# A gated mix of two attentions: Q, K and the output projected over dense features, with heads moved through DRAM

## The chip, the cores and the metric

The kernel runs on one core of one Trainium2 chip. A core has a matrix engine (PE, with a weight load that overlaps it, PEld), a vector engine (DVE), a scalar engine (ACT), a general engine (POOL) and SyncE (SP), which here only issues transfers; 16 DMA engines move the data. Each engine takes its instructions in order. The metric is the device time of one execution in microseconds (us). Before the change the median of three runs is 1757.69 us (1755.98 to 1764.59).

## The reference

Two attentions read the same `x` (2048 tokens, 640 features), and a gate mixes their outputs:

```python
g = sigmoid((x * gate_w).sum(-1, keepdims=True))
a = A_ref(x, mem0, Wq, Wk, Wv, Wo, seg_len)   # recurrent, 32 heads of 192
b = B_ref(x, wqkv, wo)                        # sliding, 32 heads of 20
out = g * a + (1 - g) * b
```

A cuts the tokens into 64 segments of 32. Each segment has 8 memory tokens in front; all 40 tokens are projected to q, k and v (640 to 6144 each), 32 heads attend with a causal mask, and the output projection gives 32 rows of the result and the next segment's 8 memory tokens. So the segments are serial.

B projects q, k, v (640 to 640 each, 32 heads of 20). Each token attends to 8 keys, its own and those 2, 4, ... 14 positions back; then comes a 640 by 640 output projection.

## The kernel before

The program has four stages: Part B (`part_b`, from L90), the prepass (L414), Part A (L509) and a last stage (L855) that finishes the rows the memory recurrence set aside. Everything is bf16 with sums in f32.

**Part B** works on the tokens in five blocks b: four of 484 and one of 112, each with 14 halo tokens in front. A block has eight steps g, each for four heads. The main loop (L296 to L331) runs through the steps (b, g) and calls:
- `make_xT(b)` (L159): transposes 512 tokens of x on PE, evicts them to `xT`, makes the gate g, copies tokens on POOL into `xh_blk` (stored to DRAM for Part A) and into `zTi`, the first eight tokens per segment, which the prepass reads. It runs at g = 2 of the block before.
- `make_v(b)` (L203): V of a block in four position groups u (two parities, two halves); at g = 6 of the block before.
- `proj(b, g)` (L220): q and k of four heads, with the features on partitions and the tokens along the row. [...] It is called one step ahead.
- `scores(b, g)` (L234): per two heads, matmuls over the 32 rows of a head (`ps_bS`), one exponential on ACT (L249), one multiplication with the band mask on DVE (L253).
- `values(b, g)` (L256), one step behind: `ps_bO`, the weighted sums, and `ps_bZ`, the sums of the weights; ACT takes logarithm and exponential of the latter (L271, L272: the reciprocal), DVE multiplies (L274) into `OT`, again 32 rows per head.
- `out_tile(ti)` (L277): output projection of 128 tokens over the eight groups of padded rows, in two halves of eight matmuls, scaled by 1 - g and stored to DRAM (`bsc_dram`). It is called from g = 1 on, when the tokens are complete.

Transposes, gate, V, q/k and the output share two PSUM banks (pool `psm`); the scores have two double banks and `psO` one bank each for O and Z. The pool `wk` gives two buffers unless a call says otherwise.

**The weights of Part A** are 80 slices of 384 KB (128 x 1536). `N_STREAM` = 14 of them are streamed anew in each segment. Of the rest, `N_EARLY` = 23 are loaded in Part B (`load_early`, L376, which also copies the 20 output slices into a contiguous DRAM buffer `wscr`), after the first `xh_blk` store. The others follow in four groups as memory becomes free (`load_late`, L399): after Part B, before the fourth q/k pass (4), before the V rounds (8) and after the prepass (4).

**The prepass** projects the 512 recurrent tokens for all segments at once and writes them to DRAM (`zpk_dram`): four passes for q and k (L434, 96 groups of five matmuls of 128 x 512), then V in four rounds of four tiles, each with 15 matmuls into three PSUM banks (L446), three evictions and two stores. `load_late(2)` (L463) puts eight slice loads on SP's queue before the first round.

**Part A** has its instruction order for PE, ACT and DVE written out by hand; for the rest, Tile's scheduler sets each engine's order from its own estimate. `load_z(s)` and `load_vz(s)` fetch one segment's prepass rows; both are issued by ACT. `load_vz(0)` stands before the loop (L544), and the later ones stand behind `store()`, after the fourth q/k group of the segment (L747).

A transfer signals one of eight semaphores that SP's and ACT's transfers use in turn; a transfer's issue waits until the one that used the semaphore before it has landed.

The functions that the change touches, with the line numbers that the profile uses:

Of the kernel before, what the change touches and what calls it, by code (L numbers as in the profile page):

```python
# [10 lines left out]
BF = mybir.dt.bfloat16  # L11
# [4 lines left out]
N_EARLY = 23  # L16
# [11 lines left out]
class _K:  # L28
# [61 lines left out]
    def part_b(self):  # L90
# [11 lines left out]
        with ExitStack() as ctx:  # L102
# [21 lines left out]
            wop = wp.tile([128, 8, 640], BF, name="wo_pad")  # L124
            wqk = [wp.tile([128, KC, 32, 32], BF, name=f"w{n}_pad") for n in "qk"]
            xT = wp.tile([128, KC, HALO + S], BF, name="xT")
            OT = wp.tile([128, 8, S], BF, name="OT")
            wsrc = self.wqkv.rearrange("(c p) f -> p c f", p=128)
            for n, w in enumerate(wqk):
                nc.gpsimd.memset(w[:, :, :, 20:32], 0.0)  # L130
                raw = OT[:].rearrange("p g t -> p (g t)")[:, 3200 * n:3200 * n + 3200]
                (nc.scalar, nc.sync)[n].dma_start(raw.rearrange("p (c f) -> p c f", c=KC), wsrc[:, :, 640 * n:640 * n + 640])
                for kc in range(KC):
                    eng = (nc.vector, nc.gpsimd)[(KC * n + kc) % 2]
                    eng.tensor_copy(w[:, kc, :, 0:20], raw[:, 640 * kc:640 * kc + 640].rearrange("p (h d) -> p h d", d=20))
            nc.sync.dma_start(gw[:], self.gate_w.rearrange("(c p o) -> p c o", p=128, o=1))
            nc.scalar.dma_start(wv[:], wsrc[:, :, 1280:1920])
            nc.gpsimd.memset(wop[:], 0.0)
            wosrc = self.wo.rearrange("(g h d) f -> h d g f", h=4, d=20)
            for hh in range(4):  # L140
                nc.sync.dma_start(wop[32 * hh:32 * hh + 20, :, :], wosrc[hh])
# [17 lines left out]
            def make_xT(b):  # L159
# [30 lines left out]
                with tc.issue_after(xh_store.ins):  # L190
                    nc.gpsimd.tensor_copy(zTi[:, :, :, 16 * b:16 * b + 16],
                                          xv[:, :, :, 24:32].rearrange("p s c i -> p c i s"))
                    if b == 3:
                        self.build_sel(self.const, sel_ones[:])
# [23 lines left out]
            qk = {}  # L218

            def proj(b, g):  # L220
                nq, nu, c0 = shape_of(b)
                nt = nq * nu
                for n, (o0, nn) in enumerate(((c0 + HALO, nt), (c0, nt + HALO))):
                    ps = bank(F32, "ps_bqk")
                    for kc in range(KC):
                        nc.tensor.matmul(ps[:, 0:nn], lhsT=wqk[n][:, kc, 4 * g:4 * g + 4, :].rearrange("p h d -> p (h d)"),  # L226
                                         rhs=xT[:, kc, o0:o0 + nn], start=(kc == 0), stop=(kc == KC - 1))
                    t = wk.tile([128, BQ + HALO], BF, name="b" + "qk"[n] + "T", bufs=3)
                    self.evac(t[:, 0:nn], ps[:, 0:nn], "dve" if n == 0 else "act")
                    qk[b, g, n] = t  # L230
# [3 lines left out]
            def scores(b, g):  # L234
                nq, nu, c0 = shape_of(b)
                nk = nq + 7
                qT, kT = qk.pop((b, g, 0)), qk.pop((b, g, 1))
                for hp in range(2):
                    ps = psS.tile([128, 2, 512], F32, tag="S", name="ps_bS")
                    for u in range(nu):  # L240
                        a = 242 * (u // 2) + u % 2
                        for r in range(2):
                            rs = slice(64 * hp + 32 * r, 64 * hp + 32 * r + 32)
# [12 lines left out]
            def values(b, g):  # L256
# [5 lines left out]
                for u in range(nu):  # L262
                    for out, z in ((pz, True), (po, False)):
                        for hh in range(4):
# [8 lines left out]
                dst = OT[:, g, BQ * b:BQ * b + nt].rearrange("p (l n q) -> p l q n", l=nu // 2, q=2)  # L273
                nc.vector.tensor_tensor(out=dst, in0=po[:, 0:nt].rearrange("p (l q n) -> p l q n", q=2, n=nq),  # L274
                                        in1=rz[:, 0:nt].rearrange("p (l q n) -> p l q n", q=2, n=nq), op=ALU.mult)

            def out_tile(ti):  # L277
                bo = io.tile([128, 640], BF, name="bo", bufs=2)
                for f in range(2):
                    ps = bank(F32, "ps_bo")  # L280
                    for g in range(8):
                        nc.tensor.matmul(ps[:, 0:320], lhsT=OT[:, g, 128 * ti:128 * ti + 128],
                                         rhs=wop[:, g, 320 * f:320 * f + 320], start=(g == 0), stop=(g == 7))
# [13 lines left out]
            with tc.issue_after(self.first_store):  # L297
                self.load_early()
            make_v(0)
            proj(*steps[0])  # L300
            ti = 0
            for i, (b, g) in enumerate(steps):
                if g == 2 and b + 1 < S // 512:
                    make_xT(b + 1)
                if (b, g) == (S // 512 - 1, 0):
# [12 lines left out]
                if g == 6 and i + 8 < len(steps):  # L318
                    make_v(b + 1)
                if i + 1 < len(steps):  # L320
                    proj(*steps[i + 1])
# [3 lines left out]
                if g >= 1 and b > 0 and 128 * (ti + 1) <= BQ * b:  # L325
# [25 lines left out]
    def weights_setup(self):  # L351
# [21 lines left out]
        self.ahead = {}  # L373
        self.wstream = self.ctx.enter_context(tc.tile_pool(name="wstream", bufs=WBUFS))

    def load_early(self):  # L376

        for k in self.early:
            self.res_tiles[k] = self.load_slice(self.wres, k, "wres_" + "_".join(map(str, k)))
        so = [k for k in self.slice_keys() if k[0] in ("oa", "ob") and k not in self.early]  # L380
        scr = self.dram.tile([len(so), 128, 1536], BF, name="wscr")
        for i, k in enumerate(so):
            src, split = self.slice_info(k)
            self.nc.sync.dma_start(scr[i].rearrange("p (c f) -> p c f", c=split[0]), src)
            self.wscr[k] = scr[i]

    def load_slice(self, pool, key, name, tag=None, t=None):
        src, split = self.slice_info(key)
        kw = {"tag": tag} if tag else {}
        if t is None:  # L390
            t = pool.tile([128, 1536], BF, name=name, **kw)
        v = t if split is None else t.rearrange("p (c f) -> p c f", c=split[0])
        if key in self.wscr:
            self.nc.sync.dma_start(t[:], self.wscr[key])
        else:
            self.nc.sync.dma_start(v[:], src)
        return v

    def load_late(self, part, side=None):  # L399
# [4 lines left out]
        for k in ks:  # L404
# [534 lines left out]
```

## Time and profile before

| what | value |
|---|---|
| median of three runs | 1757.69 us |
| profiled execution | 1761.81 us, span 1759.7 us, mean granted PE clock 0.993 |
| PE busy | 1675.3 us, 95% of the span |
| ACT, DVE, POOL busy | 872.1 (50%), 651.0 (37%), 71.3 (4%) us |
| first score matmul (L244) of blocks 0, 1, 2, 3, 4 | 31.45, 69.8, 118.3, 166.05, 207.2 us |
| first prepass matmul (L434) | 228.82 us |
| V rounds (L446), from first to last | 335.24 to 391.22 us |
| Part A's segments | from some 391 us on, about 21 us each |

The page gives the busy time of each engine and its share of the span; the chain of work that ended last, followed backward from the last instruction; and groups of instructions by line, engine, operation, output<-input and shape (partitions x elements), with their count, the busy time, the mean in ns, and the idle time before them with what ended it. Windows give the busy time of each engine in a stretch of the span, with the granted clock (1.00 is full) and the load of the DMA engines. PE pipelines its matmuls, so that the sum of their durations is more than the time they take; how far apart they start is read from the timeline.

### The profile page before, as it was taken

What the parts mean: (1) busy time and instruction counts of PE and PEld (TensorE: products, weight loads), DVE (VectorE), ACT (ScalarE), POOL (GpSimd) and SP (SyncE); (2) the same over time, 40 slices, a digit from 0 to 9 for tenths busy, and PEclk for the clock granted to TensorE, in tenths of its full rate; (3) what the DMA queues carried; (4) which work ended last, traced back from release to release, by engine and by line L of the source; (5) the groups of instructions that cost most, each with busy time, mean ns of one, the idle gap of its engine ahead of it and who ended that gap; (6) DMA issues with size and microseconds to landing.
All of it is one profiled execution on the core that took longest, in us unless ns stands there. A gap on an engine that the chain in (4) does not pass through costs nothing.

```text
span 1759.7 us, 82388 instructions
## 1 busy us (share of the span) xinstructions
PE 1675.3 (95%) x36512; PEld 998.3 (57%) x36527; DVE 651.0 (37%) x2065; ACT 872.1 (50%) x2377; POOL 71.3 (4%) x132
## 2 busy tenths in 40 slices
PE   6999999998999999999999999999999999999989
PEld 3555544445555555555555565556556655555557
DVE  4565533223333333333333333333333333333330
ACT  3766632224555555555555555555555555555550
POOL 6010000000000000000000000000000000000000
PEclk9999999999999999999999999999999999999999
DMA  6941184889999989999899999999999999998981
GB/s 172 332 125 33 40 294 120 219 248 314 298 304 293 291 282 304 308 300 304 293 295 307 298 296 308 305 297 299 304 297 306 307 297 299 301 303 296 297 286 30
DMA packets 280648, 466.50 MB, mean 265 GB/s; under 512 B 94820, under 2 KB 155748, under 8 KB 280292
## 3 DMA queue, kind: packets, MB, share of 16 engines
q1 hardware_dynamic: 178632, 401.83, 69.0%
q10 hardware_dynamic: 101660, 59.41, 11.7%
q8 instruction: 285, 4.67, 1.0%
q14 instruction: 71, 0.58, 0.1%
HBM read 427.47 MB, written 41.55 MB: 267 GB/s over the span
## 4 chain that ended last, share of the span: by engine, by line
PE 85%; ACT 6%; DMA 3%; issue 2%; DVE 2%; ACTq 0%; SPq 0%; DVEq 0%
PE ps_qk L560 25%; PE ps_v L653 13%; PE ps_wo L717 12%; PE ps_qkT L577 6%; PE ps_pre L434 6%; PE ps_S L607 5%; PE ps_oT L676 3%; PE ps_z L871 3%; PE ps_bqk L226 3%; ACT bP L249 2%; PE ps_pre L446 2%; ACT ZB L798 2%; PE ps_mem L727 1%; PE ps_bv L213 1%; PE ps_S L616 1%
## 5 line engine op out<-in xcount | busy, mean ns | idle before, releaser
L569 ACT CAST TZ<-ps_qk 128x384 bf16<-128x384 f32 x448 | 208.8, 481 | 332.3 <-PE ps_qk L560 185.5
L560 PEld LDWEIGHTS <-hT 128*32 128x32 bf16 x10240 | 246.8, 96 | 152.0 <-DVE hT L730 12.8
L584 DVE COPY ZB<-ps_qkT 128x384 bf16<-128x384 bf16 x256 | 91.6, 358 | 377.6 <-PE ps_qkT L577 212.3
L560 PE MATMUL ps_qk<-wres_q,hT 128*32 128x384 bf16 x4096 | 226.6, 328 | 2.8 <-issue 2.8
L653 PE MATMUL ps_v<-wlate_v,hT 128*32 128x384 bf16 x4096 | 224.8, 329 | 0.0
L717 PEld LDWEIGHTS <-TZ 128*32 128x32 bf16 x6144 | 154.6, 96 | 65.3 <-issue 17.4
L560 PE MATMUL ps_qk<-wlate_k,hT 128*32 128x384 bf16 x2560 | 159.8, 328 | 0.1
L560 PE MATMUL ps_qk<-wst,hT 128*32 128x384 bf16 x1792 | 153.1, 328 | 0.9 <-issue 0.7
L653 PEld LDWEIGHTS <-hT 128*32 128x32 bf16 x5120 | 113.4, 96 | 67.8 <-issue 5.1
L717 PE MATMUL ps_wo<-wlate_oa,TZ 128*32 128x384 bf16 x2560 | 140.8, 328 | 3.5 <-issue 3.4
L607 PE MATMUL ps_S<-ZB,TZ 128*128 128x160 bf16 (+1 forms) x1024 | 136.5, 237 | 0.8 <-issue 0.8
L577 PE MATMUL ps_qkT<-ident,TZ 128*128 128x128 bf16 x1536 | 130.2, 220 | 3.0 <-ACT TZ L569 2.2
L717 PE MATMUL ps_wo<-wlate_ob,TZ 128*32 128x256 bf16 x2688 | 124.5, 276 | 5.9 <-issue 5.9
L577 PEld LDWEIGHTS <-TZ 128*128 128x128 bf16 x1536 | 88.9, 98 | 64.0 <-issue 41.8
L560 PE MATMUL ps_qk<-wres_k,hT 128*32 128x384 bf16 x1792 | 119.8, 328 | 1.5 <-issue 1.1
L625 ACT ACTIVATE ZB<-ps_S 32x224 bf16<-32x224 f32 x256 | 89.4, 349 | 41.8 <-PE ps_S L616 38.7
L687 DVE CAST TZ<-ps_oT 128x192 bf16<-128x192 f32 x256 | 79.4, 351 | 61.9 <-PE ps_oT L681 61.9
L607 PEld LDWEIGHTS <-TZ 128*128 128x128 bf16 (+1 forms) x1024 | 58.8, 95 | 69.1 <-issue 41.5
L687 ACT CAST TZ<-ps_oT 128x192 bf16<-128x192 f32 x256 | 70.0, 328 | 56.1 <-PE ps_oT L681 56.1
L730 DVE CAST hT<-ps_mem 128x24 bf16<-128x24 f32 x126 | 22.5, 179 | 196.9 <-PE ps_mem L727 196.9
L660 ACT CAST TZ<-ps_v 128x384 bf16<-128x384 f32 x192 | 92.7, 483 | 3.1
L536 POOL COPY TZ<-ZB 128x384 bf16<-128x384 bf16 x64 | 32.5, 508 | 1514.4 <-DMA ZB<-zpk_dram 476.0
(142 smaller groups left out, 2443.7 us busy)
## 6 DMA issues: line engine op xcount, KB each, us to landing
wst<-in_A_Wq_dram SPq DMA_DIRECT2D x260, 384.0 KB
wst<-in_A_Wv_dram SPq DMA_DIRECT2D x260, 384.0 KB
wst<-in_A_Wk_dram SPq DMA_DIRECT2D x195, 384.0 KB
wst<-wscr SPq DMA_DIRECT2D x192, 384.0 KB
zpk_dram<-ZS ACTq DMA_DIRECT2D x4, 3072.0 KB
ZB<-zpk_dram ACTq DMA_DIRECT2D x64, 192.0 KB
wscr<-in_A_Wo_dram SPq DMA_DIRECT2D x20, 384.0 KB
wres_q<-in_A_Wq_dram SPq DMA_DIRECT2D x16, 384.0 KB
```

Source lines behind the costliest of these rows:

```text
L226: nc.tensor.matmul(ps[:, 0:nn], lhsT=wqk[n][:, kc, 4 * g:4 * g + 4, :].rearrange("p h d -> p (h d)"), rhs=xT[:, kc, o0:o0 + nn], start=(kc ...
L434: nc.tensor.matmul(ps[:], lhsT=sls[r][kc][:, c0:c0 + 128], rhs=zTi[:, kc, :], start=(kc == 0), stop=(kc == KC - 1))
L560: nc.tensor.matmul(pq[32 * j:32 * j + 32, 0:384], lhsT=hT[:, kc, :], rhs=sl[:, 384 * j:384 * j + 384], start=(kc == 0), stop=(kc == KC - 1 ...
L569: cp(sts[i], pqs[i][:, 0:384])
L577: nc.tensor.transpose(pT[:, t, :, :, :].rearrange("p j b i -> p (j b i)"), st[:, 128 * t:128 * t + 128], self.ident[:])
L584: nc.vector.tensor_copy(q_blocks(R)[:, 1:5, :, :].rearrange("p b c i -> p c b i"), pT.rearrange("p t j b i -> p (t j) b i"))
L607: nc.tensor.matmul(grid(h, par)[:, :, 0:80].rearrange("p j (b r i) -> p j b r i", r=2, i=8)[:, :, :, r, :], lhsT=KT[k0:k1, 12 * r + c:12 * ...
L625: nc.scalar.activation(E[ps], pSs[h][ps, :, 112 * j:112 * j + 112], ACT.Exp, scale=scale_a)
L653: nc.tensor.matmul(pvs[R][32 * j:32 * j + 32, 0:384], lhsT=hT[:, kc, :], rhs=sl[:, 384 * j:384 * j + 384], start=(kc == 0), stop=(kc == KC ...
L660: cp(V[R], pvs[R][:, 0:384])
L687: cps[j % 2](oTxs[2 * h + j // 2][:, 6 * (j % 2):6 * (j % 2) + 6, :], pos[j][:, 0:240].rearrange("p (c q) -> p c q", q=40)[:, :, 8:40])
L717: nc.tensor.matmul(pso[part][32 * jj:32 * jj + 32, 0:n], lhsT=oTxs[2 * (R // 2) + j // 2][:, 6 * (j % 2) + 3 * (R % 2) + t, :], rhs=o_weig ...
```

## The change

*Dense features.* The weights of q, k and the output projection are held as they come, [128, 5, 640]. `proj(b, f)` computes 128 dense features, f = 0 to 4, so a block needs 5 x 2 x 5 = 50 matmuls. A chunk of 128 features holds 6.4 heads; so that each head begins at a multiple of 32 partitions, the evicted chunk (`bqD`, `bkD`, two buffers each) is stored to a DRAM buffer, and after f = 2 and f = 4 eight loads bring half of the heads (16 heads, four steps) back as 32-row groups with 20 rows used (`bqT`, `bkT`, three buffers each). `scores` reads 20 rows. `values` writes into `boT`; after g = 3 and g = 7 four stores take it to DRAM, and after g = 7 one load brings the block's outputs back as dense features in `OT`. `out_tile` has 10 matmuls instead of 16.

*Order.* All five chunks of block 0 come before the first step; those of block b + 1 are called in steps 2 to 6 of block b. `make_xT` is called at g = 1, `make_v` at g = 7, `out_tile` from g = 3 on. The early loads are issued two per step instead of all at once, and there are 21 slices instead of 23; `wscr`'s copies follow them. POOL's copy into `zTi` no longer waits for the `xh_blk` store's issue.

*Late slices.* The eight loads of `load_late(2)` are issued one per V tile, from the fourth tile on, each after the tile's last matmul. The last four slices are issued in segment 0 after `m_qk(4)`. `load_vz` stands behind the fourth q/k group in segment 0 too.

```diff
-N_EARLY = 23
+N_EARLY = 21
...
-            wop = wp.tile([128, 8, 640], BF, name="wo_pad")
-            wqk = [wp.tile([128, KC, 32, 32], BF, name=f"w{n}_pad") for n in "qk"]
+            wo = wp.tile([128, KC, 640], BF, name="b_wo")
+            wqk = [wp.tile([128, KC, 640], BF, name=f"b_w{n}") for n in "qk"]
...
-                nc.gpsimd.memset(w[:, :, :, 20:32], 0.0)
...
-            nc.gpsimd.memset(wop[:], 0.0)
...
-            def proj(b, g):
+            heads = lambda t: t.rearrange("(g h d) n -> h d g n", h=4, d=20)
+            qk, qk_dram, ot_dram = {}, {}, {}
+
+            def proj(b, f):
...
+                    if f == 0:
+                        qk_dram[b, n] = self.dram.tile([640, nn], BF, name=f"b{'qk'[n]}_dram{b}")
                     ps = bank(F32, "ps_bqk")
                     for kc in range(KC):
-                        nc.tensor.matmul(ps[:, 0:nn], lhsT=wqk[n][:, kc, 4 * g:4 * g + 4, :].rearrange("p h d -> p (h d)"),
+                        nc.tensor.matmul(ps[:, 0:nn], lhsT=wqk[n][:, kc, 128 * f:128 * f + 128],
                                          rhs=xT[:, kc, o0:o0 + nn], start=(kc == 0), stop=(kc == KC - 1))
-                    t = wk.tile([128, BQ + HALO], BF, name="b" + "qk"[n] + "T", bufs=3)
+                    t = wk.tile([128, BQ + HALO], BF, name="b" + "qk"[n] + "D")
                     self.evac(t[:, 0:nn], ps[:, 0:nn], "dve" if n == 0 else "act")
-                    qk[b, g, n] = t
+                    nc.sync.dma_start(qk_dram[b, n][128 * f:128 * f + 128, :], t[:, 0:nn])
+                half = {2: 0, KC - 1: 1}.get(f)
+                if half is None:
+                    return
+                for n, nn in enumerate((nt, nt + HALO)):
+                    t = wk.tile([128, 4, BQ + HALO], BF, name="b" + "qk"[n] + "T", bufs=3)
+                    for hh in range(4):
+                        nc.sync.dma_start(t[32 * hh:32 * hh + 20, :, 0:nn],
+                                          heads(qk_dram[b, n][:])[hh][:, 4 * half:4 * half + 4, :])
+                    qk[b, half, n] = t
...
-                            rs = slice(64 * hp + 32 * r, 64 * hp + 32 * r + 32)
+                            rs = slice(64 * hp + 32 * r, 64 * hp + 32 * r + 20)
...
-                dst = OT[:, g, BQ * b:BQ * b + nt].rearrange("p (l n q) -> p l q n", l=nu // 2, q=2)
+                if g == 0:
+                    ot_dram[b] = self.dram.tile([640, nt], BF, name=f"bo_dram{b}")
+                if g % 4 == 0:
+                    ot_dram[b, "sb"] = wk.tile([128, 4, BQ], BF, name="boT")
+                oT = ot_dram[b, "sb"]
+                dst = oT[:, g % 4, 0:nt].rearrange("p (l n q) -> p l q n", l=nu // 2, q=2)
...
+                if g % 4 == 3:
+                    for hh in range(4):
+                        nc.sync.dma_start(heads(ot_dram[b][:])[hh][:, g - 3:g + 1, :], oT[32 * hh:32 * hh + 20, :, 0:nt])
+                if g == 7:
+                    nc.sync.dma_start(OT[:, :, BQ * b:BQ * b + nt], ot_dram[b][:].rearrange("(c p) n -> p c n", p=128))
...
-                    for g in range(8):
-                        nc.tensor.matmul(ps[:, 0:320], lhsT=OT[:, g, 128 * ti:128 * ti + 128],
-                                         rhs=wop[:, g, 320 * f:320 * f + 320], start=(g == 0), stop=(g == 7))
+                    for c in range(KC):
+                        nc.tensor.matmul(ps[:, 0:320], lhsT=OT[:, c, 128 * ti:128 * ti + 128],
+                                         rhs=wo[:, c, 320 * f:320 * f + 320], start=(c == 0), stop=(c == KC - 1))
...
-            with tc.issue_after(self.first_store):
-                self.load_early()
+            for f in range(KC):
+                proj(0, f)
             make_v(0)
-            proj(*steps[0])
-            ti = 0
+            early, ti = self.load_early(), 0
             for i, (b, g) in enumerate(steps):
-                if g == 2 and b + 1 < S // 512:
+                if g == 1 and b + 1 < S // 512:
                     make_xT(b + 1)
+                with tc.issue_after(self.first_store):
+                    for load in early[:2]:
+                        load()
+                del early[:2]
...
-                if g == 6 and i + 8 < len(steps):
+                if g == 7 and i + 1 < len(steps):
                     make_v(b + 1)
-                if i + 1 < len(steps):
-                    proj(*steps[i + 1])
+                if 2 <= g < 2 + KC and i + 8 < len(steps):
+                    proj(b + 1, g - 2)
...
-                if g >= 1 and b > 0 and 128 * (ti + 1) <= BQ * b:
+                if g >= 3 and b > 0 and 128 * (ti + 1) <= BQ * b:
...
+                if 4 * R + st >= 3 and loads:
+                    tc.add_manual_dep(loads.pop(0)().ins, mm.ins.name, self.after, reason="a load per tile")
...
-        self.load_late(2, "right")
+        loads = self.load_late(2, "right", wait=True)
...
-            load_vz(0)
...
                 if store is not None:
                     store()
-                    load_vz(s)
+                load_vz(s)
                 m_qk(4, range(KC))
+                if s == 0:
+                    for load in self.last_loads:
+                        load()
...
-    k.load_late(3)
+    k.last_loads = k.load_late(3, wait=True)
```

## The prediction

> **What bounds the kernel now.** I read the engine shares and the slices first, then the chain that ended last, and then, by windows, the stages that the change touches.
>
> ```profile
> PE 1675.3 (95%) x36512; PEld 998.3 (57%) x36527; DVE 651.0 (37%) x2065; ACT 872.1 (50%) x2377; POOL 71.3 (4%) x132
> ...
> PE 85%; ACT 6%; DMA 3%; issue 2%; DVE 2%; ACTq 0%; SPq 0%; DVEq 0%
> ```
>
> The matrix engine PE bounds the whole. Part B is the first 229 us; the table in front has its stages. Its mix, by groups of equal shape and by waits (us in total, times, longest), in 0 to 230 and 0 to 420 us:
>
> ```profile
> L249 ACT ACTIVATE bP<-ps_bS 128x968 bf16<-128x968 f32 x64 | 59.6, 985 | 0.1
> L226 PE MATMUL ps_bqk<-xT,wk_pad 128*128 128x498 bf16 x160 | 40.1, 382 | 1.0 <-ACT gz_sb L178 1.0
> L282 PE MATMUL ps_bo<-wo_pad,OT 128*128 128x320 bf16 x256 | 39.6, 304 | 0.6 <-DVE bqT L79 0.6
> L272 ACT ACTIVATE b_rz<-b_rz 128x484 f32<-128x484 f32 x32 | 19.6, 614 | 0.8
> L271 ACT ACTIVATE b_rz<-ps_bZ 128x484 f32<-128x484 f32 x32 | 19.0, 592 | 0.5 <-PE ps_bO L266 0.5
> L77 ACT CAST bkT<-ps_bqk 128x498 bf16<-128x498 f32 x32 | 18.3, 572 | 40.5 <-PE ps_bqk L226 40.5
> ...
> POOL xh_blk L185 <- DMA xh_dram<-xh_blk: 16.4, 1, 16.4
> ...
> ACT ZV L77 <- DMA wlate_ob<-wscr: 7.2, 1, 7.2
> ```
>
> Matmuls overlap, so a mean is not a price: in the timeline five projection matmuls start 1.03 us apart (205 ns each), sixteen output matmuls take 2.35 us (147 each), thirty V matmuls 4.36 (146). A plain step (66.2 to 69.9 to 73.3 us) takes 3.3 to 3.7 us: PE has 2.07 of projection, .36 of scores, .55 of values and the gaps between; ACT has two exponentials (1.86 from first start to last end), logarithm and exponential of rz (1.21) and the k eviction, some 3.5. Both are near their limit, so **PE work taken from a step does not shorten it unless ACT work goes too.** A step with an output tile takes 6.2 us (137.0, 143.2, 149.4), and there PE is the limit.
>
> Windows (PE, PEld, DVE, ACT, POOL busy; then the granted clock, DMA share, GB/s):
>
> ```profile
> 60.00:80.00 20.00, 18.64 (x307) 10.56 (x306) 12.44 (x25) 16.49 (x26) 0.00 (x0) 1.00 1.04 327
> 160.00:180.00 20.00, 17.95 (x267) 9.81 (x268) 12.99 (x23) 16.73 (x26) 0.00 (x0) 1.00 0.03 11
> ...
> 356.00:360.00 4.00, 2.25 (x11) 0.91 (x10) 1.29 (x2) 0.33 (x1) 0.00 (x0) 1.00 1.03 396
> 360.00:364.00 4.00, 3.69 (x10) 1.37 (x10) 0.01 (x1) 1.24 (x3) 0.00 (x0) 0.57 1.07 395
> ...
> 636.96:640.37 3.41, 1.93 (x85) 1.22 (x85) 0.85 (x4) 0.86 (x6) 0.00 (x0) 1.00 0.88 311
> 640.37:643.78 3.41, 3.41 (x58) 2.18 (x54) 0.18 (x1) 0.65 (x2) 0.00 (x0) 0.50 0.56 158
> ```
>
> See three things: the DMA engines are full early in Part B and empty after 140 us; PE is never under 88% in a plain stretch; and where PE was busy for only some 56% of 3 to 4 us, the next 3.41 us ran at half clock.
>
> **The change part by part.** *Removed from PE.* A full block projects with 50 matmuls instead of 80: 30 x .205 = 6.2 us; four blocks 24.6, the short block 30 x .06 = 1.8. Output: 96 of 256 matmuls x .14 = 13.4. Together 40 us. The shapes stay, so the rows are the same; score matmuls read 20 rows instead of 32, priced like L244's 32 (16 in .36; bounds .18 and .72, less than .4 us a step, under ACT's cover).
>
> *Removed elsewhere.* Per full block three k evictions on ACT (1.7 us) and three q evictions on DVE (2.0). The padding (memset L138 4.4 us and the rest on POOL, copies on DVE) lies before the first scores at 31.45; there now stand all five projections of block 0 (50 x .205 = 10.3 instead of one step's 2.1) on PE that waited for data anyway, and a trip through DRAM (7 us, below) that V's 5.8 us and the second half of the projections lie beside. I take 31.0; bounds 26 (the padding was the limit) and 38 (the trip without cover).
>
> *The order.* Compiled, the new program has PE's stream in two kinds: a block's eight head steps (scores, values) almost alone, with 10 or 20 projection matmuls between, then a lump of output, projection, V and transpose work. Before, each step carried its own projection. The walk, by rows:
> - heads: ACT 1.86 + 1.21 = 3.07 a step, eight steps 24.6. PE has .9 of this.
> - block 0: 24.6 + five k evictions 2.9 + trailing V and transposes (40 x .146 + 20 x .13 = 8.4, 1.5 beside the last step) + 4 of store waits (next part) = 38.4. Before 38.4.
> - block 1: 24.6 + .6 + lump (30 x .14 + 40 x .205 + 5.8 + 2.6 + .7 = 21.5) + 1 of store wait = 47.7. Before 48.5.
> - block 2: 24.6 + .6 + lump with ten more output matmuls 22.9 = 48.1. Before 47.8.
> - block 3: 24.6 + 1.1 + lump (40 output 5.6, short projections 1.8, short V 2.6, of which 2 beside heads) = 33.7. Before 41.2.
> - block 4 and the tail: ACT 8 x (.70 + .26 + .30) = 10 + 1.8 for its second half of q and k + 2 for the last output trip + 50 output matmuls 7.0 = 20.8. Before 21.6.
>
> Sum 31.0 + 38.4 + 47.7 + 48.1 + 33.7 + 20.8 = 219.7, so 9.1 below 228.8: of 40 us taken from PE three quarters only turn overlap into a sequence.
>
> *The clock.* A head step gives PE about .9 us of matmuls in 3.07, by the page's count (short ones overlap) 1.2, or 39%; with ten projection matmuls inside nearer 60%. The rows above go to half after 56%. So I expect half windows in the heads and at the start of each lump: .9 becomes 1.8 in a step that ACT holds at 3.07 (little), the first 3.41 us of a lump lose 1.7. I take 2 us in each of four blocks, 1 in the last: +9. Bounds: 0 and +25 (one in two windows of 125 us of heads at half, with PE work exposed each time for 1.3 us).
> [...]
>
> *Added: transfers.* Per block ten q/k stores, sixteen loads, eight stores and one load of outputs: 35 issues on SP at .33 to .45 us, 13 us of SP in a block of 40 (23 by the .66 of L312's sixteen): SP has room. The landing is what counts. Bounds for store plus dependent load: 3.8 us on an empty ring (store of g issued at 132.75, its reader at 136.54) and the 16.4 us that POOL waited for L187's store behind the resident loads, which come at one 384 KB slice per 1.0 us. From block 2 on (DMA share .03 to .2) the trip is 3.8 + 8 x .4, hidden a block ahead. In blocks 0 and 1 early slices, now two per step, share the ring; bqD and bkD have two buffers, so the third eviction waits for the first store, and DVE and ACT run in order: behind it are queued the band masks and the next exponentials, for which PE's values wait. I take 4 and 1 us; bounds 0 and 16.4 + 8. SP also waits, by the shared eight semaphores, for x loads that ACT issues; that is in the upper bound. Removing L190's ordering moves POOL's copy ahead by its store's issue, no price.
>
> *V rounds.* 335.24 to 391.22 is 56.0 us for 16 tiles of 3.24 = 51.8. Lost: 2.06 where PE waits at 358.25 for ACT's eviction, itself behind the late loads (7.2 us wait above), and 1.7 from the half window after it. Late loads released one per tile take that away: -3.5 (bounds -4.1 and +2: eight slices spread over tiles 3 to 10 are needed only in segment 0). Next late would be the streamed slices, for which PE waited 0 there. Two slices moved from early to late are 2 us of ring at 1.0 each, under the 106 us in which the prepass projects q and k, needed only after it: 0; without that cover 2.
>
> *Segment 0.* PE waits 2.22 us at 396.88 for an ACT copy held behind load_vz's issue (398.13); now that issue stands behind c_qk(3): -1.5. The wait of 1.96 for a streamed Wv slice at 405.95 stays or grows with two more late slices and the last four behind m_qk(4): bounds -2.2 and +4. The other 63 segments keep order and loads: 0, bounds ±0.1 each, as load_vz's place is the same there.
>
> Sum: -9.1 + 9 - 3.5 - 1.5 = **-5 us**. Profiled execution: 1761.8 - 5 = 1756.8; the median lies 4.1 below that execution, so **1753**.
>
> **The rivals.**
> *Forecast, no change that shows (chance .40):* 1753, 1748 to 1761.
> *Faster, full clock (.34).* Short bursts every step count as activity, or the lump overlaps with the next block's first heads. For it: the trace has seven half windows in all, though part A's 64 segments are full of short matmuls. Against: the 640.37 row. Then -9.1 - 5 = -14, 1743; with 6 us of lumps beside heads 1737.
> *Slower, store waits in blocks 0 and 1 (.18).* Third evictions wait for stores behind the resident slices. For it: the 16.4 us row. Against: loads are issued two per step, so at most some six lie ahead of a store. From 9 us beyond my 5 it cancels all; with two waits of 12 instead of 4 and 1, +19: 1772.
> *Slower, half clock throughout heads and lumps (.08).* The +25 bound: -14 + 25 = +11, 1769.
>
> **How the numbers follow.** A change under 0.5% (8.8 us) can't be told from none in this kernel. Faster: .34 and .02 from the forecast's edge, .36; slower .18 + .08 less .02 = .24; same .40. The range 1738 to 1772 leaves out a tenth on either side; the forecast's own is 1748 to 1761.
>
> **What would show it.** First scores at 31; blocks of 38, 48, 48, 34 us; prepass start at 229; PE under 50% and granted clock under .8 in head stretches, ACT over 90%; no DVE wait on q/k stores over 4 us; V rounds 52.5 us at clock 1.00. I am wrong if PE stays over 80% between 50 and 200 us (then the faster case), or if DVE or ACT waits for bq_dram or bk_dram stores add up to over 12 us.

## The result, and the profile after

The changed kernel takes 1790.47 us (median of four, 1784.15 to 1792.9) against 1759.37 for the kernel before (four runs, 1755.98 to 1764.59): 1.6% slower, ratio 1.0161 with a 95% interval of 1.0138 to 1.0184. The range of the prediction ended at 1772. The profiled executions compared below have spans of 1759.7 and 1782.3 us.

The page of the changed kernel, its parts 1, 2 and 4 (busy time; slices of the span; the chain that ended last):

```profile
span 1782.3 us, 82178 instructions
...
PE 1675.1 (94%) x36281; PEld 999.5 (56%) x36281; DVE 637.8 (36%) x2045; ACT 867.6 (49%) x2362; POOL 60.2 (3%) x124
...
PEclk9877689999999999999999999999999999999999
...
PE 86%; ACT 5%; DMA 4%; issue 3%; DVE 2%; ACTq 1%; SPq 0%; DVEq 0%
```

PE is as long busy as before, 1675.1 against 1675.3 us, although 40 us of its work are gone: the row PEclk shows why. Of the first six slices (267 us) five ran below 0.9 of the clock. In the trace, half windows (3.41 us at a granted clock of 0.50) fill 106 us of Part B, and 10 us in the kernel before. By stage, from the starts of the same matmuls in the two traces:

| stage, us | before | forecast | after |
|---|---|---|---|
| start to first scores | 31.5 | 31.0 | 35.2 |
| block 0 | 38.4 | 38.4 | 46.6 |
| block 1 | 48.5 | 47.7 | 56.3 |
| block 2 | 47.7 | 48.1 | 49.5 |
| block 3 | 40.0 | 33.7 | 40.2 |
| block 4 and tail | 22.8 | 20.8 | 27.5 |
| half clock, beside these | | 9 | (within) |
| first prepass matmul at | 228.8 | 228.7 | 255.3 |
| V rounds | 56.0 | 52.5 | 53.1 |
| first segment of Part A | 24.7 | 23.2 | 25.9 |

(Block 4 of the kernel before begins at 206.0 us, read again by its shorter score matmuls; the table in front has 207.2. So its blocks 3 and 4 are 40.0 and 22.8.) All of the loss, 26.5 us, stands before the prepass. Windows of the changed kernel, columns as in the prediction; the first four pairs are a block's heads and its lump, the last row is block 4 with the tail:

```profile
35.00:65.00 30.00, 24.23 (x372) 12.57 (x372) 16.11 (x27) 20.77 (x31) 3.64 (x3) 0.72 0.67 202
65.00:82.00 17.00, 15.36 (x150) 8.20 (x148) 7.27 (x18) 8.15 (x15) 0.00 (x0) 0.88 0.28 71
82.00:115.00 33.00, 23.98 (x427) 13.95 (x426) 18.19 (x31) 24.09 (x35) 4.08 (x3) 0.72 0.90 266
115.00:138.00 23.00, 21.49 (x154) 12.73 (x150) 9.33 (x20) 6.93 (x15) 2.31 (x2) 0.96 0.73 169
138.00:168.00 30.00, 19.82 (x397) 12.46 (x397) 16.74 (x28) 23.82 (x34) 12.62 (x42) 0.66 0.97 249
168.00:188.00 20.00, 19.94 (x116) 11.45 (x115) 6.65 (x12) 5.96 (x12) 0.00 (x0) 0.92 0.55 160
188.00:216.00 28.00, 18.34 (x372) 12.41 (x369) 14.67 (x25) 22.53 (x32) 0.00 (x0) 0.57 0.34 79
216.00:228.00 12.00, 11.65 (x113) 7.82 (x113) 4.46 (x11) 4.14 (x11) 0.00 (x0) 0.87 0.28 74
228.00:255.00 27.00, 20.01 (x252) 12.89 (x251) 9.57 (x31) 11.84 (x39) 0.00 (x0) 0.75 0.57 164
```

The two kinds of stretch are there, as read from the compiled order. The heads take 30, 33, 30 and 28 us, and in them no engine is full: PE 66 to 81%, ACT 69 to 80%, the clock 0.57 to 0.72. The DMA engines are close to it in the heads of blocks 1 and 2 (0.90 and 0.97), but not in those of block 3 (0.34), which take 28 us all the same. In the lumps PE is busy for 90 to 100% and ACT for 30 to 48%. Waits of the changed kernel, 0 to 260 us (us in total, times, longest):

```profile
ACT bP L254 <- PE ps_bS L249: 25.5, 18, 3.3
PE ps_bS L249 <- ACT bP L254: 19.5, 28, 1.8
...
ACT bo L300 <- DMA bsc_dram<-bo: 6.2, 2, 3.4
...
DVE bo L302 <- DMA bsc_dram<-bo: 4.8, 2, 2.7
ACT bkD L77 <- DMA bk_dram<-bkD: 4.4, 2, 2.8
...
DVE bqD L79 <- DMA bq_dram<-bqD: 2.5, 1, 2.5
```

ACT waits for the scores and PE's scores wait for ACT's exponentials: they take turns. The direct waits for the new stores of q and k are short (4.4 and 2.5 us; `bsc_dram` was stored before the change too). That is why the experiments had to tell two theories apart. **Order and clock:** steps without a projection leave PE and ACT taking turns at half clock. **Trips:** stores and loads hold the evictions, and with them everything behind.

### The profile page after: what moved, and what is told of

It is laid out like the page before. It is cut to its first block, busy times and chain, and to the rows that moved or that the text cites. A ratio compares the mean times of both kernels' runs of the same rounds, so it can differ in the third digit from the quotient of the medians.

```text
span 1782.3 us, 82178 instructions
## 1 busy us (share of the span) xinstructions
PE 1675.1 (94%) x36281; PEld 999.5 (56%) x36281; DVE 637.8 (36%) x2045; ACT 867.6 (49%) x2362; POOL 60.2 (3%) x124
## 4 chain that ended last, share of the span: by engine, by line
PE 86%; ACT 5%; DMA 4%; issue 3%; DVE 2%; ACTq 1%; SPq 0%; DVEq 0%
PE ps_qk L589 25%; PE ps_v L682 13%; PE ps_wo L746 11%; PE ps_qkT L606 6%; PE ps_pre L462 6%; PE ps_S L636 5%; PE ps_oT L705 3%; PE ps_z L903 3%; PE ps_pre L474 2%; PE ps_bqk L222 2%; ACT ZB L830 2%; ACT bP L254 1%; PE ps_mem L756 1%; PE ps_bv L205 1%; PE ps_bo L297 1%
## 5 line engine op out<-in xcount | busy, mean ns | idle before, releaser
L589 PE MATMUL ps_qk<-wlate_k,hT 128*32 128x384 bf16 x3072 | 180.4, 328 | 0.0
L606 PEld LDWEIGHTS <-TZ 128*128 128x128 bf16 x1536 | 88.9, 98 | 60.5 <-issue 40.5
L636 PEld LDWEIGHTS <-TZ 128*128 128x128 bf16 (+1 forms) x1024 | 58.7, 95 | 68.1 <-issue 40.2
L682 PE MATMUL ps_v<-wst,hT 128*32 128x384 bf16 x1024 | 87.1, 330 | 6.4 <-DMA wst<-in_A_Wv_dram 6.4
L589 PE MATMUL ps_qk<-wres_k,hT 128*32 128x384 bf16 x1280 | 88.6, 328 | 3.1 <-issue 2.5
```

The costliest lines, as they stand in the source:

```text
L589: nc.tensor.matmul(pq[32 * j:32 * j + 32, 0:384], lhsT=hT[:, kc, :], rhs=sl[:, 384 * j:384 * j + 384], start=(kc == 0), stop=(kc == KC - 1 ...
L606: nc.tensor.transpose(pT[:, t, :, :, :].rearrange("p j b i -> p (j b i)"), st[:, 128 * t:128 * t + 128], self.ident[:])
L636: nc.tensor.matmul(grid(h, par)[:, :, 0:80].rearrange("p j (b r i) -> p j b r i", r=2, i=8)[:, :, :, r, :], lhsT=KT[k0:k1, 12 * r + c:12 * ...
L682: nc.tensor.matmul(pvs[R][32 * j:32 * j + 32, 0:384], lhsT=hT[:, kc, :], rhs=sl[:, 384 * j:384 * j + 384], start=(kc == 0), stop=(kc == KC ...
```

## The experiments

Each kernel is the changed one with the edit shown, unless said otherwise. "Prepass at" is the start of the first prepass matmul; ratios are to the kernel before, in runs on the same chip. A trip is the way of q, k or an output through DRAM: a store, its landing, and a load.

| run | blocks 0, 1, 2, 3, 4 with tail, us | prepass at | ratio (95%) |
|---|---|---|---|
| before | 38.4, 48.5, 47.7, 40.0, 22.8 | 228.8 | 1 |
| after | 46.6, 56.3, 49.5, 40.2, 27.5 | 255.3 | 1.0161 (1.0138 to 1.0184) |
| e1 | 37.5, 57.5, 51.8, 40.5, 35.2 | 256.1 | 1.0164 (1.0133 to 1.0194) |
| e3 | 37.1, 46.9, 47.7, 40.0, 22.8 | 226.0 | 0.9996 (0.9971 to 1.0022) |
| e4 | 44.7, 64.5, 56.9, 46.9, 29.3 | 279.0 | 1.0285 (1.0245 to 1.0325) |
| e6 | 43.3, 56.8, 50.3, 40.1, 26.3 | 252.7 | 1.0160 (1.0128 to 1.0193) |
| e7 | 37.9, 57.1, 54.2, 41.5, 34.8 | 259.9 | 1.0193 (1.0154 to 1.0232) |
| e8 | 40.0, 50.7, 54.4, 41.8, 33.8 | 254.3 | 1.0168 (1.0113 to 1.0223) |
| e10 | 48.5, 60.2, 51.1, 40.3, 26.8 | 262.7 | 1.0213 (1.0164 to 1.0262) |
| e11 | 50.3, 59.2, 53.4, 31.0, 32.0 | 254.3 | 1.0153 (1.0116 to 1.0190) |
| e12 | 33.0, 41.7, 39.0, 30.6, 23.3 | 206.1 | 0.9876 (0.9844 to 0.9908) |
| e13 | 36.1, 45.2, 45.8, 40.3, 34.2 | 253.5 | 1.0141 (1.0114 to 1.0168) |
| e14 | 37.1, 39.5, 46.5, 43.5, 34.1 | 254.0 | 1.0152 (1.0103 to 1.0200) |
| e15 | 34.9, 52.8, 54.6, 43.5, 37.2 | 256.4 | 1.0159 (1.0132 to 1.0185) |
| e17 | 37.4, 45.0, 49.5, 30.4, 43.3 | 237.9 | 1.0078 (1.0051 to 1.0105) |
| e19 | 36.8, 45.8, 48.7, 38.2, 35.3 | 233.9 | 1.0039 (1.0011 to 1.0067) |
| e20 | 43.2, 56.7, 49.2, 39.3, 21.1 | 250.0 | 1.0128 (1.0057 to 1.0200) |
| e21 | 34.6, 58.8, 58.6, 49.4, 31.6 | 265.2 | 1.0227 (1.0169 to 1.0285) |
| e23 | 38.1, 44.2, 48.0, 30.5, 33.6 | 228.0 | 0.9994 (0.9974 to 1.0014) |
| e24 | 33.5, 55.4, 46.6, 35.0, 22.8 | 232.5 | 1.0023 (1.0004 to 1.0041) |

**e3, the late part on the kernel before.** `load_late(2)`, the last slices and `load_vz` as in the changed kernel, Part B as before.

> The kernel before with only the late part of the change: a late slice per V tile, the last four slices in segment 0, load_vz behind the fourth q/k group. If the two parts simply add, it is 3 to 5 us faster than before: V rounds 53 instead of 56 us, the first segment 0.5 to 1.5 us shorter, the prepass begins at 229 as before, about 1755. If the late part itself costs something in the first segment, it is within 1 us of before or slower. Part B of the changed kernel then holds all of the loss, 27 us against before at the prepass's start.

The V rounds take 52.5 us instead of 56.0, as forecast, the first segment 25.6 instead of 24.7, and the whole is no faster that these runs can tell. So Part B holds the loss. Part B of e3 is that of the kernel before, and yet its prepass begins 2.8 us earlier (226.0 against 228.8): one profiled execution differs from another by that much.

**e1, PE in program order.**

```diff
             early, ti = self.load_early(), 0
+            ctx.enter_context(tc.manual_schedule(engines={mybir.EngineType.PE}))
```

> The changed kernel, with PE's instructions in the main loop of Part B kept in the order in which the program calls them, so that each step carries its projection, output or V work again; no work is added or left out. Theory order and clock (heads alone, then a lump of long matmuls, and half clock because of it, make Part B longer): per full block 3.07 + 4.2 + 3.6 + 4 x 4.4 + 6.7 + 3.1, about 38 us instead of 47 to 56; the granted clock is 1.00 in most of Part B, the prepass begins at about 205 us instead of 255, and the time is about 1740. Rival, transfers (the trip of q and k through DRAM and the stores that evictions wait for): blocks 0 and 1 stay at 45 us and more, the waits for q/k stores and loads grow beyond 20 us, the prepass begins after 235 and the time is over 1765.

Neither: block 0 drops from 46.6 to 37.5 us, and blocks 1 and 2 rise. What had been lump is now carried by the steps, and PE stands 28.8 us in four waits for the load of OT, and the mean granted clock of the span stays at 0.969 (0.967 in the changed kernel, 0.993 before). Waits of e1, 0 to 250 us:

```profile
PE ps_bo L297 <- DMA OT<-bo_dram: 28.8, 4, 11.9
```

One cause had been covering another.

**e7, e1's edit, and the output tiles six steps after their last values.**

```diff
-                if g >= 3 and b > 0 and 128 * (ti + 1) <= BQ * b:
+                if i >= 8 * ((128 * ti + 127) // BQ + 1) + 6:
```

> As the run with PE in program order, but an output tile is called six steps after its last values instead of three (steps 6, 7 of a block and 0, 1 of the next). In that run PE stood 28.8 us in four waits for the load of OT that brings the outputs back. Theory trips: the order of PE was worth its price, but the trip of the outputs took it back; with six steps between, the waits for OT fall under 8 us, the prepass begins at 225 to 235 instead of 256, and the time is about 1762. Rival, clock and order of the other engines: the waits go, but half clock in the steps without a projection or the engines' other waits fill the place, the prepass begins after 245 and the time stays over 1775.

The waits for OT go, and PE is held elsewhere. Waits of e7, 0 to 255 us:

```profile
PE ps_bqk L222 <- DVE bqD L79: 41.8, 4, 14.6
ACT bkD L77 <- DMA bk_dram<-bkD: 41.0, 7, 12.9
DVE bqD L79 <- DMA bq_dram<-bqD: 38.4, 7, 11.4
```

Evictions of q and k wait for the stores of earlier chunks, and the projection waits for the evictions. This is the chain that the prediction priced at 5 us; in a program that doesn't wait for its own lumps it is 42.

**e12, e7 without trips.** No stores of q, k and outputs; the loads, OT's too, read Part B's weights, so that what Part B computes is meaningless.

```diff
-                    nc.sync.dma_start(qk_dram[b, n][128 * f:128 * f + 128, :], t[:, 0:nn])
...
-                                          heads(qk_dram[b, n][:])[hh][:, 4 * half:4 * half + 4, :])
+                                          heads(self.wqkv[:, 640 * n:640 * n + nn])[hh][:, 4 * half:4 * half + 4, :])
...
```

> As e7 (PE in program order, output tiles six steps later), with the stores of q, k and of the outputs left out and the 32-row groups and OT loaded from Part B's weights in DRAM, so that no eviction and no load waits for a trip; the numbers of Part B are then meaningless, the engines' work is the same. Theory trips: e7's 41.8 us in which PE waited for q evictions that waited for stores go, a full block takes 36 to 42 us, the prepass begins at 205 to 220. Rival, clock and the other engines' order: blocks stay at 47 us and more, the prepass begins after 235.

The rival falls. Prepass at 206.1, 22.7 us before that of the kernel before and 54 before e7's; the full blocks take 31 to 42. Windows of e12's blocks 1 and 2, and of block 2 of the kernel before:

```profile
71.50:113.20 41.70, 33.02 (x535) 19.50 (x534) 26.66 (x47) 31.22 (x50) 4.18 (x3) 0.92 0.71 189
113.20:152.20 39.00, 34.66 (x544) 20.79 (x544) 24.28 (x44) 28.37 (x45) 15.27 (x43) 0.91 0.83 235
...
118.00:166.00 48.00, 43.55 (x610) 25.35 (x608) 28.43 (x52) 31.66 (x52) 4.30 (x3) 1.00 0.12 30
```

The clock is at 0.91 to 0.92 and PE over 79% busy, with the DMA engines nearly as loaded as in the changed kernel (0.71 and 0.83, there 0.83 and 0.80 over blocks 1 and 2). So the smaller PE work is worth something, if the steps carry it and no trip holds them. The 22.7 us are what it is worth with trips that cost nothing; no kernel here has that with the reference's result.

**e24, without trips in the scheduler's own order** (e12's edits on the changed kernel).

> The changed kernel as the scheduler orders it, with the stores of q, k and outputs left out and the 32-row groups and OT loaded from Part B's weights, as in e12 but without e12's order of PE (Part B's numbers are meaningless). Compiled, block 0 carries its projection and V in its steps, while blocks 1 and 2 still are eight head steps and then a lump. Theory order and clock: block 0 takes 36 to 40, blocks 1 and 2 stay at 45 to 52 with the granted clock under 0.85, and Part B ends at 225 to 245. Theory trips alone: blocks 1 and 2 come down to e12's 39 to 42 in spite of the lumps, and Part B ends before 215.

As the theory of order and clock has it for the end of Part B (232.5), for block 2 (46.6) and for the clock in the heads; block 0 is shorter than it said and block 1 longer. Compiled, block 0 now carries its projection in its steps and takes 33.5 us; block 1 is still heads and lump and takes 55.4 (its heads: 72.70 to 106, clock 0.69):

```profile
39.00:72.70 33.70, 31.14 (x486) 16.88 (x485) 19.53 (x37) 25.34 (x41) 3.65 (x3) 0.90 0.69 213
72.70:106.00 33.30, 28.46 (x428) 15.99 (x427) 19.39 (x38) 26.46 (x40) 3.65 (x3) 0.69 0.70 210
106.00:128.00 22.00, 20.68 (x203) 12.09 (x201) 10.73 (x23) 8.44 (x17) 3.72 (x4) 1.00 0.59 136
```

The heads of block 1 take 33.3 us without any trip and 33 in the changed kernel: the trips are not what makes them long.

Four kernels thus give the split. With trips, order (PE's, with the output tiles later) changes little: 255.3 (scheduler), 259.9 (e7). Without trips: 232.5 and 206.1. Order costs 26 us where no trip hides it; taking the trips out gives 23 us in the one order and 54 in the other. The two are not independent: taking the trips out also changes what order the scheduler picks (13 of the 23 us are block 0, which is no longer lumped), so the 23 are not waits alone.

**e11, loads that wait for no store**, the stores kept (e12's second edit, and the same for OT, on the changed kernel).

> The changed kernel, but the loads of the 32-row groups and of OT read the weights of Part B in DRAM (same shapes and row lengths) instead of what was stored, so that they wait for no store; the stores stay. What Part B computes is then meaningless; the work is the same. Theory trips: the start, the last block and the lumps lose their waits, the prepass begins 12 us or more earlier than 255. Theory order and clock: only the first scores (35.2) and the last outputs come earlier, by 2 to 5 us each, and blocks 1, 2 and 3 stay within 3 us of 56, 50 and 40.

First scores at 28.5 instead of 35.2, prepass at 254.3 instead of 255.3: the theory of trips in this form falls. No wait of PE, ACT or DVE for a transfer of q or k is left among the longest fifty, and Part B is 1 us shorter. The compiled order is lumped again in blocks 1 and 2, which grow by 3 us each, as block 0 does by 4; block 3 gains 9 us, which the other theory did not expect either, and the tail loses 4.5.

**e4, scores and values twice.**

```diff
-                    for u in range(nu):
+                    for u in list(range(nu)) * 2:
```

> The changed kernel, with the score and value matmuls of each step issued twice (the second set starts its sums anew, so the result is the same): 0.9 us more of PE work at full clock in each of 32 long steps, 29 us in all, in stretches where ACT has 3.1 us of work a step. Theory clock: the doubled work keeps the granted clock near 1.00 in the heads, the lumps start at full clock, and Part B ends no later than 255 us, by up to 15 us earlier. Theory order alone (half clock costs little beside ACT): the clock rises too, but Part B stays within 4 us of 255 or grows. If the work simply adds, the prepass begins at 270 to 284.

Neither theory: the prepass at 279.0 is in the range named for work that simply adds. Part B grows by 23.7 us, and half windows take 116 us of it instead of 106: the clock did not rise (mean of the span 0.965, 0.967 in the changed kernel). So this run does not say what the clock costs alone; it does say that PE's work in the heads counts in full, though PE is busy for only 66 to 81% of them.

**e6, three buffers for the q and k chunks**, and **e10, x loads issued by POOL** (e8 is the same on top of e7).

```diff
-                    t = wk.tile([128, BQ + HALO], BF, name="b" + "qk"[n] + "D")
+                    t = wk.tile([128, BQ + HALO], BF, name="b" + "qk"[n] + "D", bufs=3)
```

> The changed kernel, with three buffers instead of two for each of the evicted q and k chunks. Theory transfers: the evictions' waits for the q/k stores go (4.4 us on ACT and 2.5 on DVE, and 8 us of PE in the chain before the first scores), the first scores come at 31 instead of 35.2 and the whole is 4 to 10 us faster. Theory order and clock: only the start gains, 1 to 4 us, and the blocks stay at 47 to 56.

> The changed kernel, with the loads of x from the fifth on issued by POOL instead of ACT and nothing else. Theory shared semaphores: SP's two stops of 10 us go, and blocks 0 and 1 (46.6 and 56.3 us) are 8 to 15 us shorter together. Rival, order and clock: blocks 0 and 1 keep their length within 4 us.

> As e7, with the loads of x from the fifth on issued by POOL instead of ACT. In the changed kernel SP stands still for 10 us at 54 to 65 and for 11 us at 73 to 84 in front of a transfer whose semaphore was last used by an x load that ACT issues late; everything behind it on SP, stores of q and k among it, is late by as much. Theory shared semaphores: with POOL issuing, blocks 0 and 1 together are 8 to 15 us shorter than in e7. Rival: SP's stop is covered by the block's lead; the blocks stay within 3 us of e7's.

e6: 2.6 us by the prepass, no more than e3's unchanged Part B differs; no change that shows. Of SP's two stops in the changed kernel the trace shows one to be for an x load: after 73 us SP waited 11.3 us with the issue of a slice (`SPq L417 <- DMA x_sb`, 84.23 us) for the landing of an x load that ACT had issued at 81.94 on the same semaphore (the records of the 1682 transfers of SP and ACT there name eight semaphores, 210 or 211 transfers each), and behind it, at 85.25, stood the store of a q chunk evicted by 67.71. At the other, 55 to 65, SP waited 9.4 us for DVE's eviction of q. In e10 POOL issues the x loads, and the prepass begins 7 us later, not earlier: nothing is gained by it in this order. In e8, block 1 gains 6.4 us against e7 and block 0 loses 2.1, in all 4.3, short of the 8 to 15 expected.

**e13, e14, e15, e21: queues.** e13 is e7 with three buffers and the resident slices issued by POOL (`eng=self.nc.gpsimd` in `load_slice`), where they and `wscr`'s copies no longer wait for the first `xh_blk` store; e14 adds ACT and DVE to the engines in program order; e15 is e14 with the slices on SP, behind that store as in the changed kernel; e21 adds SP to e15.

> As e7, with three buffers for the q and k chunks, and the resident slices issued by POOL, so that SP's queue in blocks 0 to 2 holds little but the trips. Theory queue (the trips are late because SP issues in order behind slices and their semaphores): the evictions' waits for stores fall from 79 us to under 20, blocks of 40 to 44, the prepass begins before 232 and the time is 1762 or less. Rival, latency of the trips themselves: waits stay over 40 us, the prepass begins after 245.

> As e13, with ACT and DVE in program order too. If the scheduler's order of ACT and DVE (eviction of q and k between the steps' exponentials) holds PE up, blocks get 2 to 5 us shorter than in e13; if not, they are within 2 us.

> As e7 with three buffers for the q and k chunks and PE, ACT and DVE in program order, slices issued by SP as in the changed kernel. Theory queue: the waits for stores stay over 30 us, blocks 1 and 2 at 50 and more, and e14 is 10 us or more faster than this. Theory order of ACT and DVE: this comes within 4 us of e14.

> As e15 (PE, ACT and DVE in program order, output tiles six steps later, three buffers), with SP in program order too, so that no transfer stands on SP ahead of one that the program issues earlier. Theory head of the line: waits for q/k stores under 25 us, blocks 1 and 2 at 38 to 46 instead of 53 and 55, the prepass begins before 235, the time is 1750 to 1768. Rival, semaphores shared with ACT's x loads and the slices in the queue: blocks 1 and 2 stay over 48.

In e13, blocks 1 and 2 fall to 45 and 46 and the waits for stores from 79 us to 41. But slices and copies now come so early that the DMA engines are full from 10 us on (share 1.02 to 1.08 up to 52 us), and the first scores stand at 51.9: the prepass begins 6 us before e7's and 2 before the changed kernel's. So the run leaves open what the queue alone would give. e14 takes 5.7 us off block 1 and loses as much elsewhere; e15 comes within 2.4 us of e14 by the prepass, as the rival of the queue had it. e21 falls: with SP in program order the waits of ACT and DVE for the q/k stores are 90.6 us. The head of SP's queue is then this:

```profile
SPq L233 <- DMA bq_dram<-bqD: 20.8, 11, 4.4
SPq L233 <- DMA bsc_dram<-bo: 15.3, 3, 8.2
SPq L290 <- DMA bo_dram<-boT: 13.8, 6, 5.1
```

SP waits for the stores of q to land before it issues their loads (L233), up to 4.4 us each, and, 15.3 us in three waits, for the landing of ACT's output stores, which these loads do not read (by the author's reading a shared semaphore, as at 84.23 us in the changed kernel); stores that are ready stand behind. None of the orders tried here avoids it.

**e19 and e20, one half of the change each**: e19 has q and k as before and the dense output, e20 the reverse (with 18 early slices, since padded outputs take more memory).

> The changed kernel with q and k projected as before (padded weights, a step's 10 matmuls one step ahead, transposes at g = 2, V at g = 6); the output stays dense, with its trip through DRAM, and the late part stays. PE has 13 us less than before. If the q/k trip and the lumps that come with it are the loss, the blocks are 38 to 48 us as before or shorter, the prepass begins at 215 to 230 and the time is 1743 to 1759. If the output's trip is the loss, the prepass begins after 240.

> The changed kernel with the output projected as before from padded rows (16 matmuls a tile, no trip for the outputs; three slices fewer fit before the prepass). PE has 13 us more than the changed kernel. If the q/k half carries the loss, the prepass begins at 250 to 268 and the time is 1780 to 1800. If the output's trip does, it begins before 242.

The q/k half carries the loss: e20 has the prepass at 250.0, with the heads and lumps of the changed kernel. The output half is 7 us ahead of the kernel before when block 4 begins (198.6 against 206.0) and loses 12.5 in the tail, so that it too misses its forecast (233.9 against 215 to 230). There PE waits 10.7 us for two trips that nothing covers, and ACT 6.9 us for the landing of a late slice (by the author's reading on a semaphore shared with the output stores). Waits of e19, 0 to 240 us:

```profile
PE ps_bo L290 <- DMA OT<-bo_dram: 10.7, 2, 5.5
...
ACT bo L293 <- DMA wlate_k<-in_A_Wk_dram: 6.9, 1, 6.9
```

**e17 and e23, output trips on POOL** (e7, three buffers, `nc.gpsimd` for the transfers of `bo_dram` and OT, whose load comes in two parts; in e23 POOL issues only those of blocks 0 to 2).

> PE in program order, output tiles six steps later, three buffers for q and k chunks, and the trip of the outputs issued by POOL instead of SP. In e13 SP stood 13.9 us in front of output stores that waited for DVE, with q/k stores behind them. Theory head of the line (SP holds stores of q and k behind stores that wait for later work): the evictions' waits for stores fall under 25 us, blocks 1 and 2 take 40 to 46, the prepass begins at 222 to 236, the time is 1755 to 1768. Rival, the shared transfers are slow in themselves: the waits stay over 40 us and the prepass begins after 245.

> As e17, but the output trips of the last two blocks go through SP again, whose queue holds little by then. In e17 the last block took 43.3 us (22.8 in the kernel before), since POOL issues a transfer in up to 6.7 us; before it, e17 was 11 us ahead of the kernel before. If POOL's issue is what the tail waits for, the last block takes 26 to 32 and the prepass begins at 220 to 227, the time 1749 to 1758. If not, it stays over 36 and the time over 1765.

e17 is the first kernel with the whole change that has block 4 begin before the kernel before has it, at 194.6 against 206.0, and gives it back at the end, where POOL's issues are slow, up to 6.7 us each. Waits of e17, 0 to 255 us:

```profile
POOL OT L291 <- issue: 24.8, 6, 6.7
POOL bo_dram L288 <- issue: 22.3, 10, 4.5
```

e23 takes 10 us of that back: prepass at 228.0, 1756.88 us, no different from the kernel before (interval 0.9974 to 1.0014), and by the two ratios some 29 us better than the changed kernel. No run with the reference's arithmetic beats the kernel before by more than can be measured.

## Why the prediction was wrong

*What was right.* The work taken off (PE's matmuls did go: for q and k of the four full blocks the trace before has 320, the one after 200), the two kinds of stretch, the lumps of blocks 1 and 2 by rows (23 and 20 us against 21.5 + 1 and 22.9; block 3's took 12 against 8), the V rounds (53.1, forecast 52.5), and that half clock would come with short bursts. The faster rival, full clock, fell: half windows fill 106 us of Part B.

*The step that failed* is "heads: ACT 1.86 + 1.21 = 3.07 a step, eight steps 24.6". The heads took 30, 33, 30 and 28, in all 121 us where the walk has 103.6 (98.4 and 5.2 of k evictions): 17 us. A sum of one engine's durations is the time of a stretch only if that engine never waits; else it is a lower bound. Here ACT was busy for 91 of the 121 us, and for most of the other 30 it waited for PE: by the trace 20.6 us for scores and some 4 for the sums, with 3.8 for transfers. The compiled order bunches the work: from 188.6 to 193 us PE has the scores of two steps with hardly any values between them, and from 199.2 to 202.8 the values of two steps with no scores. With two score tiles in PSUM and one set of sums (O, Z), each exponential then waits for scores at half clock and the next scores wait for it (25.5 and 19.5 us in all, by the waits above). That the trips are not behind it e24 shows: 33.3 us for the heads of block 1 without them. That the order is, e12 bears out: in program order and without trips block 1 takes 41.7 us where e24 has 55.4. The prediction itself named ACT over 90% as its sign; 75% was measured.

*Mis-sized:* the start by 4.2 us (q and k evictions waited for stores of 4.8 and 3.4 us in the chain, priced under V's cover); block 0's lump of 17 instead of 6.9 us beside 4 of waits; the tail by 6.7 (output tiles now stand in one row, and with two `bo` buffers an eviction waits up to 3.4 us for the store of an earlier one; before, a step lay between them). The sum: heads 17, lumps 8 (64.3 forecast with the waits, 72 measured), tail 6.7, start 4.2, less the 9 that stood for the clock, is 27 of the 26.6 us.

*The clock* was not out of proportion in the lumps, but the heads were priced as if ACT covered it ("in a step that ACT holds at 3.07 (little)"). How much of the 17 us is the clock and how much the order of scores and values stays open: e4 was meant to tell and did not.

*The slower rival by store waits* named the right chain, but the changed kernel shows 7 us of it. It becomes the bound once the order is mended (e7, 42 us).

*Segment 0:* the copy's wait went, and the wait for the streamed Wv slice, which the prediction bounded at +4, grew from 1.96 to 4.34 us; the segment is 1.2 us longer instead of 1.5 shorter.

```profile
PE ps_v L682 <- DMA wst<-in_A_Wv_dram: 4.3, 1, 4.3
```

## What to carry to other kernels

Work taken off the busiest engine is worth something only if what is left still overlaps: ask of the compiled order which engine fills each stretch, and don't price a stretch by the sum of one engine's durations unless its waits in a like stretch are near zero. A detour through DRAM adds a store, a landing and a load to every buffer's life, here on a queue where ready transfers stood behind waiting ones (a q chunk evicted by 67.71 us was stored at 85.25, behind a wait of 11.3); it needs buffers and lead for the whole trip, and a tail that has other work. When two causes cover each other, take both out in one run and then each alone, or every single repair looks useless.

## What the runs showed of the hardware that was not expected

Half clock lasted where the work was spread thin. In Part B of the kernel before, the three half windows of 3.41 us stand each alone (from 22.6, 39.6 and 84.0 us); in the changed kernel the granted clock is 0.57 over the 28 us from 188 to 216, with PE busy for 18.34 us of them by the page. In e4, with more matmuls in the same steps, half windows were no rarer (116 of 279 us, here 106 of 255). Cut into windows of 3.41 us, the changed kernel's first 262 us show half clock easier to come into than to leave: the eight windows at full clock that were followed by half clock had PE busy for 39 to 77% (others as little busy kept it), and of 31 windows at half clock only eight, with PE busy for 83 to 100%, were followed by full clock, although the same matmuls kept PE busy for longer at half clock (a score matmul 0.29 us from 192 to 219 us, 0.22 from 69 to 92.8). From 30 to 255 us no gap of PE was over 1.8 us, and the clock fell all the same.
